# An element-wise scale-and-add with a small extra store: alpha's column goes to HBM on the ACT queue

## The chip, the core and the metric

The kernel runs on one core of one Trainium2 chip. The metric is device time in microseconds (us), and lower is better. The core's engines are TensorE (PE, matrix products), VectorE (DVE, element-wise work), ScalarE (ACT), GpSimd (POOL) and SyncE (SP, which here only issues DMA transfers). Sixteen DMA engines move data between HBM, the chip's main memory, and SBUF, the on-chip memory of 128 partitions.

## What is computed

```
B, S, D = 512, 32, 640          # x and fx: [512, 32, 640] bf16, alpha: [1] bf16
def reference(x, fx, alpha):
    return x + alpha * fx
```

Each of x, fx and the output has 512 x 32 x 640 = 10,485,760 elements of 2 bytes, 20.97 MB. Two are read and one is written.

## The kernel before

The tensors are viewed as 128 partitions by 81,920 columns. The columns are cut into five units of 16,384 (`UNIT`, line 13), so that a unit of one tensor is 4.19 MB, 32 KB in each partition. Units of x are loaded in groups of two, two and one (64 KB in each partition for a group of two); units of fx are loaded one at a time.

- `load_x(u, n)` (lines 47 to 51) takes a buffer of the pool `wide`, which has two, and issues the load on SP at line 49.
- `load_f(u)` (lines 53 to 55) takes a buffer of the pool `fs`, which has two, and issues the load on SP at line 55.
- `compute(u)` (lines 57 to 66) is one DVE instruction, at line 59: x_t = f_t * a_f + x_t, written over the x buffer. Its `scalar=a_f[:]` is a column of 128 floats, one for each partition.
- `store(u, n)` (lines 68 to 71) writes a finished x buffer to the output, on SP, at line 71.

Alpha is one number in HBM. It is loaded as a single bf16 element (line 76, behind the first load of x on the same queue), multiplied on PE with a row of 128 ones (line 80), which puts it into all 128 partitions of a PSUM column, and copied by DVE to the SBUF column a_f (line 82).

The order of the instructions is written out by hand (`manual_schedule`, line 40): each engine runs its instructions in the order of lines 73 to 98. SP issues all the DMA transfers, so it waits in that order as well: a load that needs a buffer waits until the buffer has been read or stored, and what comes after it on SP waits with it. ACT has no work in this kernel.

Each transfer counts up a completion semaphore. Eight of these are used in turn, so the ninth transfer uses the first transfer's semaphore again.

Of the kernel before, what the change touches and what calls it, by code (L numbers as in the profile page):

```python
# [1 line left out]

# [4 lines left out]

ACT = mybir.ActivationFunctionType
ALU = mybir.AluOpType
F32 = mybir.dt.float32  # L10
BF16 = mybir.dt.bfloat16

UNIT = 16384
P = 128


@with_exitstack
def kernel(
    ctx: ExitStack,
    tc: tile.TileContext,  # L20
    x: bass.AP,
    fx: bass.AP,
    alpha: bass.AP,
    out: bass.AP,
):

    nc = tc.nc  # L30
    xv = x.flatten_outer_dims().rearrange("(p n) d -> p (n d)", p=P)
    fxv = fx.flatten_outer_dims().rearrange("(p n) d -> p (n d)", p=P)
    ov = out.flatten_outer_dims().rearrange("(p n) d -> p (n d)", p=P)
    assert xv.shape[1] == 5 * UNIT

    consts = ctx.enter_context(tc.tile_pool(name="consts", bufs=1))
    psum = ctx.enter_context(tc.tile_pool(name="psum", bufs=1, space=bass.MemoryType.PSUM))
    wide = ctx.enter_context(tc.tile_pool(name="wide", bufs=2))
    fs = ctx.enter_context(tc.tile_pool(name="fs", bufs=2))
    ctx.enter_context(tc.manual_schedule())  # L40

    xt, ft = {}, {}

    def cols(u, n):
        return slice(u * UNIT, (u + n) * UNIT)

    def load_x(u, n):
        t = wide.tile([P, 2 * UNIT], x.dtype, tag="x", name="x_t")
        nc.sync.dma_start(out=t[:, : n * UNIT], in_=xv[:, cols(u, n)])  # L49
        for i in range(n):  # L50
            xt[u + i] = (t, i)

    def load_f(u):
        ft[u] = fs.tile([P, UNIT], fx.dtype, tag="f", name="f_t")
        nc.sync.dma_start(out=ft[u][:], in_=fxv[:, cols(u, 1)])  # L55

    def compute(u):
        t, i = xt[u]
        nc.vector.scalar_tensor_tensor(  # L59
            out=t[:, i * UNIT : (i + 1) * UNIT],  # L60
            in0=ft[u][:],
            scalar=a_f[:],
            in1=t[:, i * UNIT : (i + 1) * UNIT],
            op0=ALU.mult,
            op1=ALU.add,
        )

    def store(u, n):
        t, i = xt[u]
        assert i == 0  # L70
        nc.sync.dma_start(out=ov[:, cols(u, n)], in_=t[:, : n * UNIT])

    load_x(0, 2)

    a_1 = consts.tile([1, 1], alpha.dtype, name="a_1")
    nc.sync.dma_start(out=a_1[:], in_=alpha[None, :])  # L76
    ones = consts.tile([1, P], alpha.dtype, name="ones")
    nc.vector.memset(ones[:], 1.0)  # L78
    a_ps = psum.tile([P, 1], F32, name="a_ps")
    nc.tensor.matmul(a_ps[:], ones[:], a_1[:], start=True, stop=True)  # L80
    a_f = consts.tile([P, 1], F32, name="a_f")
    nc.vector.tensor_copy(out=a_f[:], in_=a_ps[:])  # L82

    load_f(0)
    load_f(1)
    load_x(2, 2)
    compute(0)
    load_f(2)
    compute(1)
    store(0, 2)  # L90
    load_f(3)
    load_x(4, 1)
    compute(2)
    load_f(4)
    compute(3)
    store(2, 2)
    compute(4)
    store(4, 1)


# [1 line left out]
_INS = ['x', 'fx', 'alpha']  # L102
_OUTS = [((512, 32, 640), 'bfloat16')]


# [23 lines left out]
```

## Time and profile before

| what | value |
|---|---|
| time, median of 3 runs | 152.76 us (152.31 to 152.86) |
| the profiled execution's own time | 152.47 us |
| its span, first to last instruction | 150.7 us |
| DVE busy | 86.7 us (58%) |
| the five big DVE instructions (line 59) | 86.3 us, 17.28 us each |
| DMA moved | 62.92 MB, mean 418 GB/s |
| HBM read and written | 41.94 MB and 20.97 MB |

The profiler records when each instruction starts and ends on its engine, what it waited for, and every packet of the DMA engines. The page has the busy time of each engine, the DMA queues, the chain of work that ended last, and the costliest groups of instructions. Other views of the same trace list the waits, the instructions in order of time, and the busy time in chosen stretches of the span. Times in these views are us from the start of the span.

The groups of big instructions start in this order: units 0 and 1 at 32.77 us, back to back; unit 2 at 72.24; unit 3 at 101.17; unit 4 at 120.77. The first store is issued at 67.28 us, the second at 118.48, and the last at 138.1, which takes 11.6 us to land.

### The profile page before, as it was taken

Reading aid. Unit: us, or ns where it says so; the run is one execution under the profiler, and the core shown is the slowest. Engines: PE = TensorE matmul, PEld = TensorE weight load, DVE = VectorE, ACT = ScalarE, POOL = GpSimd, SP = SyncE. Lnnn points to the kernel's source line nnn. Section 1 sums busy time; section 2 is a strip of 40 time slices with the busy share of each in tenths; the row PEclk is TensorE's granted clock in tenths of the full one; section 3 lists DMA queues with packets and bytes.
Section 4 is the critical chain, followed back from the end, with each engine's and each line's share of the span. In section 5 each row is a group of like instructions: output and inputs, shape, how many; then the busy total and the mean of one; then the engine's idle time right before and its main releaser. Section 6 shows DMA issues by size and latency. Waiting matters only on the chain.

```text
span 150.7 us, 75 instructions
## 1 busy us (share of the span) xinstructions
PE 0.2 (0%) x1; PEld 0.1 (0%) x1; DVE 86.7 (58%) x7; POOL 0.2 (0%) x4
## 2 busy tenths in 40 slices
PE   0000000000000000000000000000000000000000
PEld 0000000000000000000000000000000000000000
DVE  0000000039999999980899970019999499996000
POOL 0000000000000000000000000000000000000000
DMA  8899899999999896999899989999999999989993
GB/s 278 383 452 470 365 418 417 426 426 444 478 452 487 348 557 278 426 452 478 348 522 417 417 365 418 435 418 426 444 435 470 487 435 400 470 365 391 435 426 139
DMA packets 1586, 62.92 MB, mean 418 GB/s; under 512 B 178, under 2 KB 178, under 8 KB 178
## 3 DMA queue, kind: packets, MB, share of 16 engines
q1 hardware_dynamic: 1586, 62.92, 97.5%
HBM read 41.94 MB, written 20.97 MB: 417 GB/s over the span
## 4 chain that ended last, share of the span: by engine, by line
DMA 56%; DVE 34%; SPq 1%; issue 0%; DVEq 0%
DMA f_t<-in_fx_dram 40%; DVE x_t L59 34%; DMA out_dram<-x_t 16%; SPq L49 0%; SPq L76 0%; DVEq L59 0%; SPq L55 0%
## 5 line engine op out<-in xcount | busy, mean ns | idle before, releaser
L59 DVE SCALAR_TENSOR_TENSOR x_t<-f_t,a_f,x_t 128x16384 bf16<-128x16384 bf16 x5 | 86.3, 17284 | 29.0 <-DMA f_t<-in_fx_dram 29.0
L82 DVE COPY a_f<-a_ps 128x1 f32<-128x1 f32 x1 | 0.2, 157 | 21.6 <-PE a_ps L80 21.6
L78 DVE MEMSET ones<- 1x128 bf16 x1 | 0.2, 165 | 0.8 <-PEq L113 0.8
L80 PE MATMUL a_ps<-a,ones 1*128 1x1 bf16 x1 | 0.2, 158 | 22.4 <-DMA a<-in_alpha_dram 22.4
L113 POOL MEMSET const-uint8-127<- 128x1 uint8 x1 | 0.1, 102 | 0.0
L113 POOL MEMSET const-bfloat16-1.0<- 128x1 bf16 x1 | 0.1, 101 | 0.0
L80 PEld LDWEIGHTS <-ones 1*128 1x128 bf16 x1 | 0.1, 98 | 1.0 <-DVE ones L78 1.0
L113 POOL MEMSET const-float32-0.0<- 128x1 f32 x1 | 0.1, 98 | 0.2 <-issue 0.2
L113 POOL MEMSET const-float32-1.0<- 128x1 f32 x1 | 0.1, 98 | 0.0
## 6 DMA issues: line engine op xcount, KB each, us to landing
f_t<-in_fx_dram SPq DMA_DIRECT2D x5, 4096.0 KB, 32.3
x_t<-in_x_dram SPq DMA_DIRECT2D x1, 4096.0 KB, 19.4
out_dram<-x_t SPq DMA_DIRECT2D x1, 4096.0 KB, 11.6
x_t<-in_x_dram SPq DMA_DIRECT2D x2, 40.5
out_dram<-x_t SPq DMA_DIRECT2D x2, 22.8
a<-in_alpha_dram SPq DMA_DIRECT2D x1, 0.0 KB
```

Source lines behind the costliest of these rows:

```text
L59: nc.vector.scalar_tensor_tensor(out=t[:, i * UNIT : (i + 1) * UNIT], in0=ft[u][:], scalar=a_f[:], in1=t[:, i * UNIT : (i + 1) * UNIT], op ...
L78: nc.vector.memset(ones[:], 1.0)
L80: nc.tensor.matmul(a_ps[:], ones[:], a_1[:], start=True, stop=True)
L82: nc.vector.tensor_copy(out=a_f[:], in_=a_ps[:])
L113: nc = _bacc.Bacc("TRN2", target_bir_lowering=False, num_devices=1)
```

## The change

A second memory pool, in HBM, is opened, and right after a_f has been computed it is also stored to a scratch tensor of 128 floats in that pool. The store is issued by ACT, so on ACT's DMA queue, and nothing reads the scratch tensor. The rest of the kernel is as before.

```
+    hbm = ctx.enter_context(tc.tile_pool(name="hbm", bufs=1, space=bass.MemoryType.DRAM))
...
     a_f = consts.tile([P, 1], F32, name="a_f")
     nc.vector.tensor_copy(out=a_f[:], in_=a_ps[:])
+    a_hbm = hbm.tile([P, 1], F32, name="a_hbm")
+    nc.scalar.dma_start(out=a_hbm[:], in_=a_f[:])
 
     load_f(0)
     load_f(1)
```

More of the change, by code (lines that the diff above doesn't have):

```diff
@@ L37 @@
     psum = ctx.enter_context(tc.tile_pool(name="psum", bufs=1, space=bass.MemoryType.PSUM))
+    hbm = ctx.enter_context(tc.tile_pool(name="hbm", bufs=1, space=bass.MemoryType.DRAM))
     wide = ctx.enter_context(tc.tile_pool(name="wide", bufs=2))
@@ L82 @@
     nc.vector.tensor_copy(out=a_f[:], in_=a_ps[:])
+    a_hbm = hbm.tile([P, 1], F32, name="a_hbm")
+    nc.scalar.dma_start(out=a_hbm[:], in_=a_f[:])
     load_f(0)
```

## Prediction

> **What bounds the kernel now.** I read the DMA lines of the page first, then the waits of the vector engine (DVE) and of the issuing queue (SP), then the timeline, then busy time by stretch. The page's DMA part:
>
> ```profile
> DMA packets 1586, 62.92 MB, mean 418 GB/s; under 512 B 178, under 2 KB 178, under 8 KB 178
> ## 3 DMA queue, kind: packets, MB, share of 16 engines
> q1 hardware_dynamic: 1586, 62.92, 97.5%
> ```
>
> One queue, and its packets fill 97.5% of the time of all 16 DMA engines: 0.975 x 150.7 = 146.9 of 150.7 us. The packet count can be taken apart: eleven big transfers of 128 rows are 1408 packets; the 178 small ones are alpha itself and 177 semaphore updates (16 for each big transfer, one for alpha). So a 128-row transfer is split 8 rows to an engine, with one update behind them.
>
> ```profile
> DVE x_t L59 <- DMA f_t<-in_fx_dram: 29.0, 4, 11.6
> ```
>
> This is the DVE's largest wait, of the view of waits: it is the transfers that DVE waits for. Its five big instructions are 86.3 us of 150.7. The stretches between the hand-overs, in the view of busy time by stretch (length; busy of PE, weight load, DVE, POOL; clock; DMA share; GB/s):
>
> ```profile
> 22.40:32.80 10.40, 0.16 (x1) 0.00 (x0) 0.19 (x2) 0.00 (x0) 1.00 1.00 432
> 32.80:67.30 34.50, 0.00 (x0) 0.00 (x0) 34.45 (x2) 0.00 (x0) 1.00 1.01 435
> 67.30:91.50 24.20, 0.00 (x0) 0.00 (x0) 17.28 (x1) 0.00 (x0) 1.00 1.00 425
> 91.50:118.50 27.00, 0.00 (x0) 0.00 (x0) 17.28 (x1) 0.00 (x0) 1.00 1.00 430
> 118.50:138.10 19.60, 0.00 (x0) 0.00 (x0) 17.29 (x1) 0.00 (x0) 1.00 1.01 436
> ```
>
> Look at the last two columns: from 22.4 to 138.1 us the DMA share is 1.00 in every stretch. Nothing hides behind a gap, so time that is added to the DMA engines after 22.4 us moves the end one for one. Time added anywhere else costs nothing unless it empties that queue.
>
> **The change, part by part.** It removes nothing and moves nothing: in the built order of instructions PE, DVE, POOL and SP have the same instructions in the same sequence, and ACT has one more, the store of the column, between its two branches. The timeline says when it starts:
>
> ```profile
> 22.41 0.16 PE L80 MATMUL a_ps<-a,ones 1*128 1x1 bf16 x1 [22.41 <-DMA a<-in_alpha_dram]
> 22.61 0.16 DVE L82 COPY a_f<-a_ps 128x1 f32<-128x1 f32 x1 [21.63 <-PE a_ps L80]
> 32.77 34.48 DVE L59 SCALAR_TENSOR_TENSOR x_t<-f_t,a_f,x_t 128x16384 bf16<-128x16384 bf16 x2 [10.01 <-DMA f_t<-in_fx_dram]
> ```
>
> a_f is ready at 22.61 + 0.16 = 22.77 us. The store issues then, in the midst of the load of f_t 0.
>
> 1. The wait it adds is ACT's for the DVE copy. Nothing is queued behind it on ACT but the branch to the end, and nobody waits for ACT before the end. Cost 0, hidden by an idle engine. The issue itself takes 0.32 to 0.84 us in the rows of SP's issues, on ACT's own sequencer; SP's next issue is at 50.08 us, so the two don't meet.
>
> 2. The engines' work: 128 runs of 4 B on 16 engines, 8 each, and one update, 9 packets an engine. There is no store of that size in this trace. The nearest row is the 2 B packet of alpha: 9 ns in the trace's packet records; the 4 B semaphore updates have 9 ns too. 9 x 9 ns = 0.08 us on each engine. That is the lower end for the work itself. The upper end is that an engine stands still until each of its small writes is confirmed. In the trace's records the last data packet of the kernel ends at 149.33 us and its semaphore has arrived at 149.67: 0.35 us for a confirmation with nothing else in flight. 8 x 0.35 = 2.8 us. I take 0.1 (0.08 rounded up), because both rows of small packets stand near it and because the updates that close the eleven transfers today open no visible gap: eight of the eleven transfers end within the stretches of 1.00 above. Both ends go into the range.
>
> 3. Can it gain? Transfers could by chance fall better. If the stretches of 432, 435, 425 and 430 GB/s all ran at 436, they would shrink by 10.40 x 4/436 + 34.50 x 1/436 + 24.20 x 11/436 + 27.00 x 6/436 = 0.10 + 0.08 + 0.61 + 0.37 = 1.2 us. So -1.2 is the lower end; I take 0, for nothing in the store would raise a rate.
>
> 4. Semaphores. The transfers' completion semaphores are eight, used in turn. The new store takes one place in the turn, so later transfers shift by one. In the built order two waits are new on SP: the load of x_t for unit 4 waits for alpha's semaphore as well, and the store of units 2 and 3 waits for the column's store as well. The first has been fulfilled since 22.4 us when SP gets there; a separate wait instruction takes some 0.06 us (five in a row at the end of the trace stand 0.06 us apart), and it delays a load that queues behind f_t 3, which was issued at 67.68 and lands at about 101.1, while the load is issued at 91.48: cover of 9.6 us, cost 0. The second is rival C. SP's list of waits shows what is behind it:
>
> ```profile
> SPq L71 <- DVE x_t L59: 62.1, 3, 26.1
> ```
>
> Without cover the second would hold back the store of units 2 and 3 and, behind it on SP, the last store. The count of semaphores at the end stays ten, so the final waits stay.
>
> Sum against the profiled execution: span 150.7 + 0.1 = 150.8; with the 1.77 us around the span (152.47 - 150.7), 152.57. The median of the three runs is 152.76, 0.29 above the profiled one: 152.86, so **152.9 us**.
>
> **A rule against the change.** No run here shows a small write to HBM. The Trainium skill, page "DMA: Bandwidth & Descriptors", Specifications, gives 512 B as the least transfer for line rate and says that below it the DMA engine reads, modifies and writes; its section "Latency and other measured facts" gives an HBM access 0.2 us on average and 2 us under high load. If the eight writes of an engine were taken one after the other with one such read each, an estimate from that page is 8 x 0.2 = 1.6 us to 8 x 2 = 16 us, against 0.08 by the 9 ns row: 154.4 to 168.8 instead of 152.9. The page doesn't say that the engine stands still meanwhile.
>
> **The rivals.**
>
> A, the forecast: the packets pass between the big ones. 152.9, with 152.3 (the fastest of the runs before is 152.31) to 153.5.
>
> B, slower: the 4 B writes hold their engine. One place, the load of f_t 0 from 22.8 us on; one price, up to 0.35 us each, 2.8 us; 152.76 + 2.8 = 155.6. It decides the sign from 0.76 / 8 = 0.095 us a write on (0.76 us is 0.5% of 152.76, which is about what a measurement of this kernel can tell from no change). For it: all 128 runs go to one 512 B piece of HBM, and every engine is loaded, so no idle time takes it up. Against it: 9 ns rows, and the absence of gaps when a queue passes from loads to stores. Half-way, 0.17 us a write, it gives 154.1.
>
> C, slower: the store of units 2 and 3 waits for the column's store. It decides from a landing after 118.48 us, where SP issues that store now, and each us later is a us more. Landing as I work it out: 22.8 + about 1.1 (from the first issue at 0.73 to the first packet at 1.78 us) + 9 turns, if one small packet gets in after each 32 KB packet of 1.21 us, = 34.8 us. That is 84 us early.
>
> D, slower: a second queue costs time outside the transfers, at start or end. For it: 152.47 - 150.7 = 1.77 us lie around the span of a kernel with one queue, and nothing shows what they are. If that doubled, 154.5. Against it: the instructions at the start and the end are the same, and the store is long over at the end.
>
> E, faster: the stages run closer to 436 GB/s, at most -1.2: 151.6. For it only that rates differ among stages.
>
> F, the change doesn't do what it says: the scratch tensor is read by nobody, but the built order has the store on ACT. The time would be 152.76.
>
> **How the numbers follow.** A 0.60, F 0.01 (same time); B 0.22; D 0.08; C 0.01; E 0.08. Slower by over 0.5% is B, C and D: 0.31. Faster by over 0.5% is E: 0.08. Within: 0.61. The time is that of A, 152.9. The range takes in the bounds of steps 2 and 3, from E's 151.6 to B's 155.6; what it leaves out, a cost beyond B's price or a late landing as in C, is under 2 in 10. A's own range is 152.3 to 153.5.
>
> **What would show it.** In the changed kernel a second queue in the page's part 3 with 144 packets (128 + 16) and a share of about 9 x 9 ns / 150.8 us, under 0.1%. ACT's issue at about 22.8 us, landing between 24 and 35 us. The stretch from 22.4 to the start of the first big DVE instruction is 10.4 us: in A it stays under 10.9, in B it grows by up to 2.8 and every later start shifts by as much. In D all starts stay and the span or the time around it grows. In C SP's waits name the column's store, and the issue at 118.48 moves alone. I am wrong about the price of a packet if the new queue's share is over 0.5%, and about the whole reading if the big packets (1.21 us for 32 KB) get slower while the small ones take nothing.

## The result and the profile after

The changed kernel takes 157.49 us (median of 6 runs, 156.46 to 157.88) against 152.59 us for the kernel before in the same comparison (152.15 to 152.86). The ratio is 1.0315, 95% interval 1.0298 to 1.0332: 4.9 us slower. The range on record ended at 155.6 us, so the time lies outside it.

The DMA part of the page after the change:

```profile
DMA packets 1730, 62.92 MB, mean 404 GB/s; under 512 B 322, under 2 KB 322, under 8 KB 322
## 3 DMA queue, kind: packets, MB, share of 16 engines
q1 hardware_dynamic: 1586, 62.92, 97.6%
q10 hardware_dynamic: 144, 0.00, 0.1%
```

The second queue has the 144 packets that were expected, and they occupy 0.1% of the engines. The big packets of q1 still fill 97.6%, of a span that is now 155.8 us. By these lines nothing has happened; only the mean rate, 404 instead of 418 GB/s, shows that the same packets took longer.

The timeline after (start, length, engine, line, what, idle before; lines left out are marked):

```profile
22.40 0.16 DVE L83 COPY a_f<-a_ps 128x1 f32<-128x1 f32 x1 [21.42 <-PE a_ps L81]
22.59 0.34 ACTq L85 DMA_DIRECT2D a_hbm<-a_f  x1
36.85 34.48 DVE L60 SCALAR_TENSOR_TENSOR x_t<-f_t,a_f,x_t 128x16384 bf16<-128x16384 bf16 x2 [14.29 <-DMA f_t<-in_fx_dram]
...
77.43 17.29 DVE L60 SCALAR_TENSOR_TENSOR x_t<-f_t,a_f,x_t 128x16384 bf16<-128x16384 bf16 x1 [6.10 <-DMA f_t<-in_fx_dram]
...
106.42 17.29 DVE L60 SCALAR_TENSOR_TENSOR x_t<-f_t,a_f,x_t 128x16384 bf16<-128x16384 bf16 x1 [11.71 <-DMA f_t<-in_fx_dram]
```

The line of unit 2 before:

```profile
72.24 17.28 DVE L59 SCALAR_TENSOR_TENSOR x_t<-f_t,a_f,x_t 128x16384 bf16<-128x16384 bf16 x1 [4.99 <-DMA f_t<-in_fx_dram]
```

The first big DVE instruction starts 4.1 us later than before (36.85 against 32.77), that of unit 2 is 5.2 us later (77.43 against 72.24), that of unit 3 also 5.2, and so it stays to the end. All the time is lost between 22 and some 45 us. Busy time by stretch of 5 us, before and then after (last two columns: DMA share, GB/s):

```profile
27.00:32.00 5.00, 0.00 (x0) 0.00 (x0) 0.00 (x0) 0.00 (x0) 1.00 1.02 439
32.00:37.00 5.00, 0.00 (x0) 0.00 (x0) 4.23 (x1) 0.00 (x0) 1.00 1.00 433
```

```profile
22.00:27.00 5.00, 0.16 (x1) 0.00 (x0) 0.16 (x1) 0.00 (x0) 1.00 1.00 433
27.00:32.00 5.00, 0.00 (x0) 0.00 (x0) 0.00 (x0) 0.00 (x0) 1.00 0.99 282
32.00:37.00 5.00, 0.00 (x0) 0.00 (x0) 0.15 (x1) 0.00 (x0) 1.00 1.03 210
37.00:42.00 5.00, 0.00 (x0) 0.00 (x0) 5.00 (x1) 0.00 (x0) 1.00 0.94 288
42.00:47.00 5.00, 0.00 (x0) 0.00 (x0) 5.00 (x1) 0.00 (x0) 1.00 1.03 446
```

The line from 32 to 37 us is the one to learn from: the DMA share stays at 1 and the rate halves, from 433 to 210 GB/s. An engine whose packet stands still counts as busy; the GB/s tell. Both columns book a whole packet where it starts, so a stretch that is hardly longer than its packets can show a share far above or below 1.

The trace's packet records make the account. An undisturbed packet of 32 KB takes 1.213 us and one of 64 KB 2.418 us. I add up what all big packets took beyond that and divide by the 16 engines; call it the **stall**. Before it is 1.57 us in the whole span, after 6.70 us: 5.13 more, and the span is 5.1 us longer. The time in which the engines had no packet hardly changed, 3.7 us of the span before and 3.6 after. Of the 6.70, 5.71 lie between 24 and 44 us, where before has 0.00. So the loss is in the big packets, up to 4.2 us for one of 32 KB; the small ones are 9 ns each, as assumed. They come one at a time, each after a 32 KB packet of its engine, 1.21 us apart. The first two small packets of an engine pass freely; from about 29 us on the big packets of all 16 engines are slow at once.

### The profile page after: what moved, and what is told of

Same layout as the page of the kernel before. It is cut to its first block, busy times and chain, and to the rows that moved or that the text cites. A ratio compares the mean times of both kernels' runs of the same rounds, so it can differ in the third digit from the quotient of the medians.

```text
span 155.8 us, 77 instructions
## 1 busy us (share of the span) xinstructions
PE 0.2 (0%) x1; PEld 0.1 (0%) x1; DVE 86.7 (56%) x7; POOL 0.2 (0%) x4
## 3 DMA queue, kind: packets, MB, share of 16 engines
q1 hardware_dynamic: 1586, 62.92, 97.6%
## 4 chain that ended last, share of the span: by engine, by line
DMA 57%; DVE 33%; SPq 1%; issue 0%; DVEq 0%
DMA f_t<-in_fx_dram 41%; DVE x_t L60 33%; DMA out_dram<-x_t 16%; SPq L50 0%; SPq L77 0%; DVEq L60 0%; SPq L56 0%
## 6 DMA issues: line engine op xcount, KB each, us to landing
a_hbm<-a_f ACTq DMA_DIRECT2D x1, 0.5 KB, 19.6
```

## The experiments

The theories of the first four runs. S: the 128 writes hinder each other because they fall into one 512 B piece of HBM. R: every write to HBM below 512 B is dear, wherever it goes. T: the second queue is dear. Edits are against the changed kernel. Except in pitch512 only the added lines are shown; the store or load in them replaces the changed kernel's store.

**pitch512**

```
-    a_hbm = hbm.tile([P, 1], F32, name="a_hbm")
-    nc.scalar.dma_start(out=a_hbm[:], in_=a_f[:])
+    a_hbm = hbm.tile([P, 128], F32, name="a_hbm")
+    nc.scalar.dma_start(out=a_hbm[:, :1], in_=a_f[:])
```

> The same 128 writes of 4 B from the ACT queue, each now at the start of its own 512 B of HBM (a scratch tensor of 128 x 128 floats, of which one column is written). Theory S (the writes of the changed kernel hinder each other because all lie in one 512 B piece): no stall is left, 152.7 us, within 0.3 of the kernel before. Theory R (every write to HBM that is smaller than 512 B costs its engine about 5.1 / 8 = 0.64 us, wherever it goes): 157.5 us as in the changed kernel. Theory T (a second queue beside the loaded one costs a change-over at each of its packets): 157.5 us too.

Measured: 152.33 us beside 152.36 for the kernel before, ratio 0.9998 (0.9986 to 1.0009); stall from 24 to 44 us 0.00. The same packets from the same queue at the same time, and nothing is lost: R and T fall, S holds. The stretch that fell to 210 GB/s:

```profile
32.00:37.00 5.00, 0.00 (x0) 0.00 (x0) 4.33 (x1) 0.00 (x0) 1.00 1.01 433
```

**wide512**

```
+    a_w = consts.tile([P, 128], F32, name="a_w")
+    nc.vector.tensor_copy(out=a_w[:], in_=a_ps[:].to_broadcast([P, 128]))
+    a_hbm = hbm.tile([P, 128], F32, name="a_hbm")
+    nc.scalar.dma_start(out=a_hbm[:], in_=a_w[:])
```

> Each partition stores 512 B instead of 4 B on the ACT queue, at the same moment, from a tile of 128 x 128 floats that DVE fills with alpha (one more DVE copy). Same number of packets. Theory S: every write has its own 512 B, so no stall; the 65 KB themselves are 0.15 us at 436 GB/s: 152.9 us. Theory R: no write below 512 B is left, so 152.9 us too. Theory T: the change-overs remain, 157.5 us.

Measured: 152.51 beside 152.36 us, ratio 1.0011 (1.0000 to 1.0022). 128 times the bytes, no loss. Against T again.

**on_sp**

```
     load_x(2, 2)
+    nc.sync.dma_start(out=a_hbm[:], in_=a_f[:])     # instead of the store on ACT
     compute(0)
```

> The column's store is issued by SP instead of ACT, after the load of x_t for units 2 and 3, so its eight packets stand one behind the other on each engine, behind that load, at about 61 us, with the load of f_t 2 behind them. Theory S and theory R: the writes are the same, so the cost is the same, some 5 us, 157 to 158 us, seen at 61 us instead of at 29 us. Theory T: there is no second queue, so 152.7 us.

Measured: 157.30 beside 152.36 us, ratio 1.0319 (1.0303 to 1.0334). There is no second queue and the loss is the same; it has moved to 61 us, where one 32 KB packet takes up to 7.2 us. The stretch from 62 us before, and three after:

```profile
62.00:67.00 5.00, 0.00 (x0) 0.00 (x0) 5.00 (x1) 0.00 (x0) 1.00 1.00 433
```

```profile
57.00:62.00 5.00, 0.00 (x0) 0.00 (x0) 5.00 (x1) 0.00 (x0) 1.00 1.09 347
62.00:67.00 5.00, 0.00 (x0) 0.00 (x0) 5.00 (x1) 0.00 (x0) 1.00 1.09 138
67.00:72.00 5.00, 0.00 (x0) 0.00 (x0) 0.31 (x1) 0.00 (x0) 1.00 0.68 249
```

**small_load**

```
+    a_l = consts.tile([P, 2], BF16, name="a_l")
+    nc.vector.tensor_copy(out=a_l[:], in_=a_ps[:].to_broadcast([P, 2]))
+    nc.scalar.dma_start(out=a_l[:], in_=xv[:, :2])  # instead of the store
```

> ACT issues a load instead of the store: the first 4 B of each partition's row of x go from HBM to a 128 x 2 bf16 tile in SBUF that DVE has just written from alpha's PSUM column, so at the same moment. Alpha's column isn't stored. Theories S and R are about writes to HBM: 152.7 us. Theory T: 157.5 us. If every transfer of 4 B runs is dear in either direction: 157.5 us as well, and wide512 then tells the two apart.

Measured: 152.39 beside 152.36 us, ratio 0.9993 (0.9983 to 1.0002). 128 loads of 4 B cost nothing. They lie 160 KB apart, one partition's share of x, so loads that crowd weren't tried. After these four runs the cause is the place of the writes: pitch512 changes only where the writes land, and the loss is gone.

The next question was how near is too near.

**pitch64** and **pitch16**: `hbm.tile([P, 16], F32)` and `hbm.tile([P, 4], F32)`, of which the first column is written.

> The 128 writes of 4 B from ACT lie 64 B apart, so eight share each 512 B. The 512 B apart cost nothing; how large is the piece of HBM in which the writes hinder each other? If it is 512 B or more and each write behind another in the same piece costs the same: 112 of 128 still do, some 4.4 us, 156.7 us. If it is 64 B or less: 152.4 us as at 512 B. If it is 512 B but different pieces are served beside each other, eight in a row hide behind the packets between them, and this run can't tell it from 64 B: 152.4 us.

> The writes lie 16 B apart, so four share each 64 B and 32 share each 512 B. Pieces of 512 B, one write after the other in each, pieces beside each other: 32 in a row instead of 128, a quarter of 5 us at the most, 152.4 to 153.6 us. Pieces of 64 B: four in a row instead of 16, also a quarter at the most, 152.4 to 153.6. If the price were paid for every write that has a neighbour within 64 B or within 512 B, whatever their number: 156 to 157.4 us.

Measured: 152.26 us, ratio 1.0004 (0.9989 to 1.0020), and 152.25 us, ratio 0.9993 (0.9978 to 1.0009), beside 152.27. Both have a stall of 0.00 from 24 to 44 us. 16 B apart is enough here, and having a neighbour within 64 B isn't dear in itself.

**half64**

```
+    a_hbm = hbm.tile([64, 1], F32, name="a_hbm")
+    nc.scalar.dma_start(out=a_hbm[:], in_=a_f[:64, :])
```

> Only the first 64 of the 128 partitions are stored (the other half of alpha's column isn't), 4 B apart, in 256 B. If the price is paid for every write, whatever the size of the piece, half of 5 us: 154.9 us. If what counts is how many writes fall into one 64 B (still 16) and each such line has its own row of waiting writes, the engines wait as long as with 128: 157.3 us.

Measured: 159.15 beside 152.27 us, ratio 1.0447 (1.0421 to 1.0473). Neither expectation came true: half the writes cost more than all of them, stall 7.30 us. The page of half64, share and rate in 40 slices:

```profile
DMA  8969989909999996979989969999999999996993
GB/s 267 500 300 534 400 384 417 267 33 217 409 425 484 434 534 300 500 334 467 534 367 434 534 300 425 417 459 417 434 417 459 409 534 400 400 534 267 459 467 142
```

In the ninth slice (31.4 to 35.4 us) the share is 0 and 33 GB/s are left. The engines aren't idle there: packets of up to 6.5 us, which are booked where they started, run through the slice, and almost none of the whole core's traffic moves on to a new packet. A fixed price for each write is ruled out.

**row512**

```
+    r_ps = psum.tile([1, P], F32, name="r_ps")
+    nc.tensor.matmul(r_ps[:], a_1[:], ones[:], start=True, stop=True)
+    a_r = consts.tile([1, P], F32, name="a_r")
+    nc.vector.tensor_copy(out=a_r[:], in_=r_ps[:])
+    a_hbm = hbm.tile([1, P], F32, name="a_hbm")
+    nc.scalar.dma_start(out=a_hbm[:], in_=a_r[:])
```

> The same 512 B with the same content in HBM, but out of one partition: PE puts alpha into a row of 128 columns in one partition, DVE copies the row, ACT stores it. It adds a small matrix product and uses few packets, 1 to 16 of 32 to 512 B, instead of 128 of 4 B. Theory S (writes that share a piece are served one after the other): at most 16 instead of 128 writes in the piece, so at most 5 / 8 = 0.6 us, 152.4 to 153.0. If the price belonged to the 512 B being written at all from a second queue: 157.3 us.

Measured: 152.18 beside 152.27 us, ratio 0.9988 (0.9973 to 1.0003). The same 512 B of data arrive in HBM as one packet of 512 B, which takes 27 ns in the records. It is the way to do the changed kernel's job for nothing.

**pitch8**, **shift16**, **n16**: `hbm.tile([P, 2], F32)` with its first column written; `hbm.tile([P + 4, 4], F32)` with `a_hbm[1 : P + 1, :1]` written; and `hbm.tile([16, 1], F32)` from `a_f[:16, :]`.

> The 128 writes of 4 B lie 8 B apart, between the 4 B that cost 5 us and the 16 B that cost nothing. Theory X (what costs is that writes of different DMA engines meet in one 64 B line; an engine takes four neighbouring rows in turn, which at 16 B fill just one line): 8 rows to a line, so two engines meet, and the stall is there, 154 to 159 us. Theory X32 (the same with 32 B): four rows to 32 B, one engine, 152.3 us. Theory D (what costs is two writes within 16 B, whoever makes them): two rows to 16 B, 154 to 159 us. Theory D8 (two writes within 8 B): 152.3 us.

> The writes lie 16 B apart as in the run that cost nothing, but start 16 B further on, so that the four neighbouring rows of an engine lie across two lines and every line has rows of two engines. Theory X and X32: the stall comes back, 154 to 159 us. Theories D and D8: nothing changed but a place, 152.3 us.

> Only the first 16 of the 128 partitions are stored (the rest of alpha's column isn't), 4 B apart, in 64 B, one write to an engine. Theory X, X32 and D: the writes meet in one line at about the same time, so a stall remains, but as each engine has only one write out, and two in the changed kernel passed before the first long packet, the engines may pass over it: 152.3 to 155 us. A price for each write (45 ns of all engines): 16 x 0.045 = 0.7 us, 153.0 us.

Measured beside 152.37 us: pitch8 153.31, ratio 1.0063 (1.0029 to 1.0097); shift16 152.30, ratio 1.0000 (0.9985 to 1.0014); n16 152.59, ratio 1.0010 (0.9993 to 1.0027). By the times, theory X falls with shift16, and pitch8's loss of 0.9 us fits neither theory D (154 us or more) nor D8 (none). The packet records see more: the stall from 24 to 44 us is 1.19 us in pitch8, 0.54 in shift16 (0.00 in pitch16, which differs only by the shift) and 1.46 in n16, with only 16 writes. The profiles of pitch8 and n16 are each of one run that isn't typical: n16's is the slowest of its ten (153.13 us), pitch8's is faster than its median (152.79). So n16's stall goes with a loss of some 0.8 us and not with the 0.2 of its median; the give-back that is told below makes up part of the rest.

**late** (a_g is one more SBUF column like a_f)

```
     compute(4)
+    nc.vector.tensor_copy(out=a_g[:], in_=a_f[:])
+    nc.scalar.dma_start(out=a_hbm[:], in_=a_g[:])   # instead of the early store
     store(4, 1)
```

> The column's store waits until the last big DVE instruction is done (DVE then copies the column once more, and ACT stores the copy), so it runs beside the last two stores to the output instead of beside loads. If the stall holds all the engines' traffic, whatever its direction: 156 to 159 us. If it holds only reads from HBM: 152.4 us. The column's own landing may also stick out at the end by itself.

Measured: 157.37 beside 152.37 us, ratio 1.0332 (1.0299 to 1.0365). The time lost is the same, and from 138 us on only stores are under way, so stores are held up as well as loads. The first line is before, the others are late:

```profile
143.00:148.00 5.00, 0.00 (x0) 0.00 (x0) 0.00 (x0) 0.00 (x0) 1.00 1.00 433
```

```profile
138.00:143.00 5.00, 0.00 (x0) 0.00 (x0) 0.26 (x2) 0.00 (x0) 1.00 1.02 406
143.00:148.00 5.00, 0.00 (x0) 0.00 (x0) 0.00 (x0) 0.00 (x0) 1.00 0.86 223
148.00:153.00 5.00, 0.00 (x0) 0.00 (x0) 0.00 (x0) 0.00 (x0) 1.00 0.77 210
```

The 5.1 us by which the span grew are made up otherwise here. The stall from 138 us on is 3.32 us (before 0.06), with 32 KB packets of up to 2.4 us, and the last big packet ends 3.9 us later than before. Another 1.1 us lie behind it: the last part of the output lands 1.30 us after its last packet instead of 0.35, and the column's own landing is what SP waits for at the end, 0.2 us behind the output's:

```profile
SPq L129 <- DMA a_hbm<-a_g: 16.1, 1, 16.1
```

The last six runs put the store on SP, at the place of on_sp, where the writes of an engine come all at once and not 1.2 us apart. The theories were M (writes for one 64 B line that are under way together are taken one after the other), D (the distance as such counts) and X (writes of different engines in one line).

**sp_pitch16**, **sp_pitch32**, **sp_pitch64**: `hbm.tile([P, 4], F32)`, `[P, 8]` and `[P, 16]`, the first column written.

> The column is stored by SP behind the load of x_t for units 2 and 3, as in the run on SP that cost 4.9 us, but 16 B apart. All eight writes of an engine come at once, so the four rows of a 64 B line come at once. Theory M (writes for one line that are under way together are taken one after the other): a stall of a quarter of that run's, 1.2 us, 153.6 us; anything from 152.9 to 157 is for M. Theory D (distance as such) and theory X (different engines in one line): none, 152.3 us.

> The same on SP, 32 B apart: two rows to a 64 B line. Theory M with 64 B lines: an eighth of 4.9 us at the most, 152.3 to 152.9 us. Theory M with lines of 512 B or more (16 rows in one): as much as with 64 B lines 4 B apart, 157 us. Theory D: 152.3 us.

> The same on SP, 64 B apart: every write has its own 64 B line, eight share 512 B. Theory M with 64 B lines, and theory D: 152.3 us. Theory M with lines of 512 B: eight at once, about half of 4.9 us, 154.7 us. If a burst of 128 small writes costs something wherever they go: above 152.9 us.

Measured beside 152.39 us: 152.43, ratio 1.0004 (0.9992 to 1.0016); 152.46, ratio 1.0000 (0.9987 to 1.0014); 152.26, ratio 0.9994 (0.9982 to 1.0006). M's 153.6 us for sp_pitch16 is refuted as a time. Its stall, from 58 to 66 us, is 0.54 us; that of the other two is 0.01 and 0.00. Its stretch, where before has 433 GB/s:

```profile
62.00:67.00 5.00, 0.00 (x0) 0.00 (x0) 5.00 (x1) 0.00 (x0) 1.00 0.96 367
```

**sp_half64**: the 64 partitions of half64, at the place of on_sp.

> The same on SP, 4 B apart, but only the first 64 partitions (the other half of alpha's column isn't stored): four lines of 16 writes instead of eight. Lines served one after the other, so a price for each write: half of 4.9 us, 154.8 us. Lines served beside each other: the length of one line's row of 16 writes counts, as in the full column, 157.3 us.

Measured: 156.12 us (155.11 to 157.03) beside 152.39, ratio 1.0259 (1.0216 to 1.0302). It lies between the two expectations: four times 64 B with 16 writes each cost 3.7 us, eight times cost 4.9. Its profile is of the fastest of its four runs (155.11 us).

**sp_shift16** and **sp_wide16**: the tile of shift16 on SP; and a tile `[P, 4]` of alpha stored whole, 16 B a partition without gaps, on SP.

> The column is stored by SP in one burst, 16 B apart as in the run on SP that cost nothing, but begun 16 B further on, so that by theory X two engines write into each 64 B line at once. Theory X: a stall of 1 us or more, above 153.3 us. Theory D (two writes within 8 or 16 B): 152.4 us.

> Every partition stores 16 B instead of 4, one behind the other in HBM without gaps, by SP in one burst (DVE fills a tile of 128 x 4 floats with alpha first). Theory D: each 16 B has one write, 152.4 us. If it is the touching of neighbours, at whatever width below 512 B, that costs: 155 to 157.4 us.

Measured beside 152.47 us: 152.61, ratio 1.0011 (0.9995 to 1.0026), and 152.53, ratio 1.0006 (0.9996 to 1.0017). Stalls 0.36 and 0.60 us, like sp_pitch16's. The 1 us or more of theory X don't come on SP either. Touching neighbours aren't dear; 64 B with four writes are alike, whether these leave gaps or not.

The runs that store the column in writes of 4 B, by the number of writes that share 64 B if the scratch tensor begins on a multiple of 64 B, which no record shows (stall from 24 to 44 us on ACT, from 58 to 66 us on SP, from 138 us on in late). The stall is of one profile each and the ratio of all runs:

| run | queue | writes | B apart | writes in 64 B | ratio | stall, us |
|---|---|---|---|---|---|---|
| the change | ACT | 128 | 4 | 16 | 1.0315 | 5.71 |
| half64 | ACT | 64 | 4 | 16 | 1.0447 | 7.30 |
| n16 | ACT | 16 | 4 | 16 | 1.0010 | 1.46 |
| late | ACT | 128 | 4 | 16 | 1.0332 | 3.32 |
| on_sp | SP | 128 | 4 | 16 | 1.0319 | 5.07 |
| sp_half64 | SP | 64 | 4 | 16 | 1.0259 | 3.36 |
| pitch8 | ACT | 128 | 8 | 8 | 1.0063 | 1.19 |
| pitch16, shift16 | ACT | 128 | 16 | 4 | 0.9993, 1.0000 | 0.00, 0.54 |
| sp_pitch16, sp_shift16 | SP | 128 | 16 | 4 | 1.0004, 1.0011 | 0.54, 0.36 |
| sp_pitch32 | SP | 128 | 32 | 2 | 1.0000 | 0.01 |
| sp_pitch64 | SP | 128 | 64 | 1 | 0.9994 | 0.00 |
| pitch64, pitch512 | ACT | 128 | 64, 512 | 1 | 1.0004, 0.9998 | 0.00, 0.00 |

What is shown: separate writes that crowd into a few tens of bytes of HBM hold up all of the core's transfers, loads and stores alike, and the price climbs faster than the crowding (2, 4, 8, 16 writes in 64 B: 0.01, up to 0.54, 1.19, 5.07 to 5.71 us for 128 writes beside loads). It isn't the count of writes in 512 B: n16 has 16 there and stalls for 1.46 us, sp_pitch32 has 16 too and 0.01, and pitch16, on n16's queue, has 32 and 0.00. Nor is it the 512 B tensor itself: row512 fills one with a single write at no loss.

What stays open: whether the piece is 64 or 32 B (sp_pitch32 has one write in each 32 B, sp_pitch16 two); whether nearness in time or the meeting of different engines is what hurts at 16 B (pitch16 and shift16 differ by 0.54 us in one profile each, while on SP the shift makes no such difference; the trace doesn't show which engine writes which row); and why 64 writes stall for longer than 128 on ACT (7.30 against 5.71) and for less on SP (3.36 against 5.07; by the median times 3.7 against 4.9 us lost). What happens in the memory itself no record shows.

## Why the prediction was wrong

**The step that failed is step 2**, the price of the engines' work. Its lower end was right about the packets (9 ns each, queue share 0.1%) and wrong as a price, since packet time isn't where the cost appears. Its upper end failed in its reasoning: "an engine stands still until each of its small writes is confirmed", eight times 0.35 us. This holds each engine up for its own writes, one by one, with the confirmation of an idle moment. The runs show another thing: 5.13 us are lost in the big packets of all 16 engines, which are slow together, and it isn't their own confirmations that they wait for. In n16 all semaphore updates of the store, which is what step 2 takes for the confirmation, have arrived by 28.9 us, while big packets are slow until 32.7. The writes interfere with each other, so no row of a single small write could bound them, neither alpha's 2 B load (a load; small_load shows that 128 loads of 4 B that lie far apart are free) nor the semaphore updates. For the price of many writes side by side the trace of before has no row at all, and an end of 2.8 us was too sure.

**The choice within step 2** failed with it: the value was put at the near row, 0.1 us, though the cause that decided stood in the text under B ("all 128 runs go to one 512 B piece of HBM"). B had the right sign and nearly the right place, the load of f_t 0 from 22.8 us on (the slow packets run from 28.9 to 42.3 us and reach into the load of f_t 1), but 2.8 us where 5.13 were lost; the first big DVE start moved by 4.1 us and not "by up to 2.8".

**What held.** No gap hides anything: the added stall of 5.13 us went into the span one for one. Nothing queues behind ACT's wait; the issue is at 22.59 us and takes 0.34. C didn't come: the store landed 19.6 us after its issue, at 42.2, instead of 34.8, but far ahead of the second store. In pitch512, without a stall, it landed 13.2 us after an issue at 22.93, so at 36.1. The turn-taking was as assumed, except that the first small packet went out at 26.0 us and not at 23.9. D is out: the time around the span is 157.58 - 155.8 = 1.78 us against 1.77. E is out. The last sentence of the prediction named the sign that appeared: the big packets got slower and the small ones took nothing.

**The rule that spoke against the change** was right about the direction and not about the cause. The Trainium skill, page "DMA: Bandwidth & Descriptors", Specifications, ties the full rate to the size of a transfer, 512 B or more, and says nothing there of the place. pitch512, pitch64, pitch16 and sp_pitch32 make 128 writes of 4 B each, at ratios from 0.9993 to 1.0004. That 5.1 us fell into the 1.6 to 16 us that were estimated from the page is no support: by that estimate these four runs would have lost as much.

## What to carry to other kernels

Don't store a column of single 4 B values, one from each partition, side by side in HBM while transfers matter: 512 B cost 5 us here. Turn it into a row in one partition first (row512), or put the values at least 32 B apart (16 B cost no time here, but showed a stall of up to 0.54 us). When a DMA-bound kernel slows down and the share of the DMA engines stays at 1, look at the GB/s by stretch and at the longest packets. Where small transfers are added, count how many writes go to the same few bytes before pricing them one by one.

## What the runs showed that was not expected

- Fewer writes can cost more: 64 partitions 159.15 us, 128 partitions 157.49, on the same queue.
- A small stall is partly given back. Before, the big packets lose 0.50 us between 66 and 76 us, just behind the issue of the first store. In the runs with a stall between 24 and 44 us (the change, half64, pitch8, n16, shift16) that loss is 0.00 to 0.02 us; in those without (pitch512, wide512, small_load, pitch64, row512) it is 0.31 to 0.62, with pitch16 an exception at 0.06. So up to 0.5 us of a stall doesn't show in the time, as in shift16. What causes that loss, and why it then goes, wasn't tried.
- The first packet of the second queue started 3.4 us after its issue (26.0 against 22.59), while the first load of the kernel started 1.0 us after its own (1.74 against 0.73; the prediction read 1.78, and its other two packet times are 0.04 us high as well, which moves none of its sums by more than 0.1 us).
